# A fused attention and router kernel: the late plan one tick earlier, one GpSimd drain instead of two, later inverse norms, and one product moved to GpSimd

## The chip, the cores and the metric

The kernel runs on one core of a Trainium2 chip. The metric is device time in microseconds (us). A core has five engines with a queue each: TensorE (PE; its weight loads are shown as PEld), VectorE (DVE), ScalarE (ACT), GpSimd (POOL) and SyncE (SP, which here issues the plain DMAs). GpSimd issues the indirect DMAs, which gather or scatter rows by a list of row numbers. An engine works its queue in order; it waits on semaphores for what others make.

## The reference

Two stages. The first is a linear attention with sketched features, the second a router that sends every token to one of eight experts.

```python
# attention: q, k, v are [4, 4, 1088, 32], S1 and S2 are [8, 32]
phi(x) = outer product of (S1 x) and (S2 x), flattened to 64
kv  = einsum('bhsf,bhsd->bhfd', phi(k), v)
z   = sum over s of phi(k)
out = (phi(q) @ kv) / (phi(q) @ z + 1e-6)
# router: x = out as [4352, 128], 8 experts, hidden width 1024
xn, en  = x / (|x| + 1e-6), emb / (|emb| + 1e-6)
logits  = xn @ en.T / tau
e       = argmax(logits)
gate    = softmax(logits)[e]
out[t]  = gate[t] * (relu(x[t] @ w1[e]) @ w2[e])
```

## The kernel before

**Stages.** The four batches are worked as two halves, m = 0 and m = 1. For each half the keys of 17 groups of 128 tokens are turned, sketched and multiplied into `kp`, and summed into `kv`; then the queries are turned, sketched, multiplied into their features `qp`, and multiplied with `kv`. This gives the tokens' rows `x` and their logits, which go to a DRAM table `rows`. Each half has its queries in steps of four groups (c0 = 0, 4, 8, 12) and one of a single group (c0 = 16).

**The router in blocks.** Tokens are sorted by expert into 36 blocks of 128. Each block is gathered by an indirect DMA (`fetch`, L881), turned by TensorE (`turn`, L887, with a copy `xTb`, L889), multiplied with the expert's w1 (`up`, L935), passed through relu by ScalarE (`hT`, L943), multiplied with w2 (`down`, L971), scaled by the gate (`y`, L977) and scattered to the output by an indirect DMA (L980). In blocks 30 to 33 two experts share a block (L940, L974), with a second copy of w2 that ScalarE makes (`second_weights_b`, L922).

**The gate.** `norm` squares and sums a row on ScalarE (L948) and takes the root on GpSimd (L949, a power of 0.5). `inverse` adds a small number and takes the reciprocal on VectorE (L952, L953). `shares` is the exponential with its sum on ScalarE (L959), `share` the reciprocal of that on VectorE (L962, L963).

**Two plans.** Which token goes to which row of which block is worked out on the chip. The first plan covers m = 0 and gives blocks 0 to 9 (`EARLY` is 10), so that they can begin while m = 1's queries are still worked. The late plan covers both halves and gives blocks 10 to 35. It is made of small VectorE steps: `count` (per expert), `rest` (running sums, L814 to L823 and L700), `shared` (L829 to L844), `others` (L705 to L858), `experts` (L865 to L869), `find` (L740: compare each token's place with each row of each block), `high` and `low` (L744: two products with the digits of the token numbers). TensorE sums them (`sums`, L750, 34 small matmuls), and `tokens` (L765 to L767) makes the lists `dst_i` and `src_i` for the indirect DMAs. `first_rows` and `halves` add the blocks that two experts share. `mark` (L674) makes the table that the sums have as weights.

**Order.** It is written by hand. Every piece is put at a tick and a rank: `put_at(tick)(after, rank, f)`; the pieces are emitted by tick, then rank, and each engine gets its instructions in that order. Block i has tick 10 + i (`first` is 10), so block 10 is in tick 20 and is turned in tick 19. In tick 10 + i stand, by rank: fetch of block i + 4 (29), up (30), turn of block i + 1 (45), the inverse of some later block (46), shares (60), share (73), down of block i - 1 (74), a norm of some later block (74.6), the loads of w1 for block i + 2 (79). The late plan has ticks 13 to 18 (`table1` is 12, and it is put at `table1` + 1 to + 6). Blocks 10 to `known` + `AHEAD` are fetched right after it; those after them four ticks ahead.

**Norms.** The norm of block i stands in the tick of block i - 3, its inverse one tick later; for blocks 10 to 12 one tick ahead and in the tick of the block. The last block's norm stands at rank 29.2 of its tick, ahead of `up`.

**Drains.** In ticks 28 and 42 (blocks 18 and 32) GpSimd has a drain at rank 29.5 (L1092): it goes on only when it has nothing under way.

**Queries of m = 1.** They are placed by a table of their own: step by step `tr` (turn q), `ab` (sketch), `b` (copy of the second factor), `prod` (`features`, L385), `tr_qp` (L537), `qpT` (L542), `nd` (L550) and `x` (L560 to L567). [...] `tr_qp` and `nd` use two rotating PSUM buffers (`ps_big`), as `up` does.

Of the kernel before, what the change touches and what calls it, by code (L numbers as in the profile page):

```python
# [48 lines left out]
EARLY = (NM * NC * P // 2 - E * (P - 1) + P - 1) // P  # L49
LATE = NBLK - EARLY  # L50
SHARED = E // 2
PAIRS = FULL - EARLY
AHEAD = 4
USUAL = N // P + 2
# [9 lines left out]
def kernel(  # L64
# [13 lines left out]
    nc = tc.nc  # L78
# [8 lines left out]
    def ps_small():  # L87
        return psum.tile([P, 512], F32, tag="t", bufs=2, name="ps_t")

    def ps_big():  # L90
        return psum.tile([P, 2, 512], F32, tag="big", bufs=2, name="ps_big")
# [121 lines left out]
    ps = ps_small()  # L213
# [264 lines left out]
    def queries(m, c0, c1, put, put_nd):  # L478
        n = c1 - c0
        w = n * P  # L480
        s = {}
# [11 lines left out]
        def ab():  # L493
            s["ab"] = sketch(ab_bank(put.tick, n, 0), s["qT"], n)

        by_pool = m == 1 and c0 == 0

        def b():
            if by_pool:
# [20 lines left out]
        def seconds(j):  # L520
            if j == 0:
                s["b"] = tile_of(n, [P, 2, w], "qpT")
                s["qpT"] = held[:, c0 // 4].rearrange("p (a n) -> p a n", a=2)
            nc.scalar.copy(s["b"][:, j].rearrange("p (j n) -> p j n", j=2), s["big"][j][:, :, 2 * P:])  # L524
# [3 lines left out]
                                 s["big"][j][:, :, :2 * P].rearrange("p j (a n) -> p j a n", a=2),  # L528
                                 s["b"][:, j].rearrange("p (j a n) -> p j a n", j=2, a=2))

        def tr_qp(half=None):
            if half != 1:
                s["ps"] = ps_big() if n > 1 else ps_small().rearrange("p (b n) -> p b n", b=2)
            ps = s["ps"]
            for j in range(n) if half is None else range(2 * half, 2 * half + 2):
                for p in range(2):
                    nc.tensor.transpose(ps[:, p, j * P:(j + 1) * P],  # L537
                                        s["qp"][:, j, 2 * p:2 * p + 2].rearrange("p h f -> p (h f)"), ident)
# [31 lines left out]
        if m == 0:  # L570
            put(-1, 53, tr)
            if n == 1:
                put(0, 50, ab)
                put(0, 50.5, b)
                put(0, 54, prod)
                for f in (tr_qp, qpT):
                    put_nd(-1, 57, f)
            else:
                put(0, 50, pairs)
                for j in range(2):  # L580
                    put(0, 50.5, lambda j=j: seconds(j))
                    put(0, 54, lambda j=j: prods(j))
            put_nd(0, 70, nd)
            put_nd(0, 71.5 if n == 1 else 71, x)
        else:

            at_rank = ({tr: (7, 53), ab: (7, 70.6), b: (7, 70.7), prod: (7, 71.2), tr_qp: (8, 55.5), qpT: (8, 58),
                        nd: (8, 84), x: (8, 90)},
                       {tr: (8, 53.5), ab: (8, 55.8), b: (8, 58.7), prod: (8, 62.5), tr_qp: (9, 20), qpT: (9, 20),
                        nd: (9, 30), x: (9, 71)},  # L590
                       {tr: (8, 55.3), ab: (8, 84.6), b: (8, 84.7), prod: (9, 20.2), (lambda: tr_qp(0)): (9, 30.2),
                        (lambda: tr_qp(1)): (9, 30.22), qpT: (9, 30.6),
                        nd: (10, 70), x: (10, 71)},
                       {tr: (8, 84.5), ab: (9, 21), b: (9, 30.7), prod: (10, 33), tr_qp: (11, 20), qpT: (11, 20),
                        nd: (11, 70), x: (11, 71)})[min(step, 3)]
            for f, (t, rank) in at_rank.items():
                put_at(t)(0, rank, f)
        if c1 == s1:

            by = 1 if m == 0 else 2  # L600
            bank = (lambda: spare[m, 4 + 4 * by]) if c1 < NC else (lambda: table_bank[m][:, 0])
            best, pick, place, take, split, mark, write = router(m, s0, s1, g, bank)

            if m == 0 and c1 < NC:
                at_rank = {best: (0, 80), pick: (0, 81), place: (1, 70.5), take: (1, 71.2), split: (2, 54),
                           mark: (2, 54), write: (1, 55)}
            elif m == 0:
                at_rank = {best: (0, 80), pick: (0, 81), place: (1, 56), take: (1, 56.9), split: (1, 57),
                           write: (0, 82), mark: (1, 59)}
            elif c1 < NC:  # L610
                at_rank = {best: (1, 72), pick: (1, 72), write: (1, 90), place: (2, 70.5),
                           take: (2, 71.2), split: (4, 76.5), mark: (5, 76)}
            else:
                at_rank = {best: (1, 31), pick: (1, 31), place: (2, 31), take: (2, 32), split: (2, 32),
                           write: (1, 90), mark: (6, 32)}
            if c1 == NC:
                put_nd(at_rank[place][0], at_rank[place][1] - 0.1, lambda: table_bank.append(ps_big()))
            for f, (t, rank) in at_rank.items():
                put_nd(t, rank, f)
# [255 lines left out]
    def of(i):  # L875
        return (0, i) if i < EARLY else (1, i - EARLY)

    def fetch(i):
        t, j = of(i)
        xs[i] = work.tile([P, ROW], F32, tag="xs", bufs=AHEAD + 2, name="xs")  # L880
        nc.gpsimd.indirect_dma_start(  # L881
            out=xs[i][:], out_offset=None, in_=rows[:2 * S if t == 0 else N],
            in_offset=bass.IndirectOffsetOnAxis(ap=src_i[t][:, j:j + 1], axis=0))
# [23 lines left out]
    def two(i):  # L907
        return FULL <= i < FULL + SHARED
# [36 lines left out]
    def norm(i):  # L945
        sq = work.tile([P, DM], F32, tag="sq", bufs=1, name="sq")
        norms[i] = work.tile([P, 1], F32, tag="norm", bufs=6, name="norm")
        nc.scalar.activation(sq, xs[i][:, :DM], ACT.Square, accum_out=norms[i])  # L948
        nc.gpsimd.tensor_tensor(out=norms[i], in0=norms[i], in1=half_c, op=ALU.pow)  # L949

    def inverse(i):
        nc.vector.tensor_scalar_add(norms[i], norms[i], NORM_EPS)  # L952
        nc.vector.reciprocal(norms[i], norms[i])  # L953
# [36 lines left out]
    def put_at(tick):  # L990
        def put(after, rank, f):
            at.setdefault(tick + after, []).append((rank, len(at.get(tick + after, ())), f))
        put.tick = tick
        return put
# [15 lines left out]
    count, rest, others = plan_early()  # L1010
    find, high, low, sums, tokens, *_ = table(0, 1, lambda: early["key"])
    put = put_at(ND_AT[0][-1] + 1)
# [13 lines left out]
    first = ND_AT[0][-1] + 3  # L1026
# [3 lines left out]
    count, rest, shared, others, experts = plan_late()  # L1030
    find, high, low, sums, tokens, first_rows, halves = table(1, NM, lambda: late["key"])
    table1 = ND_AT[1][-1] + 1
    put = put_at(table1)
    put(1, 31.5, count)
    put(2, 75, rest)
    put(1, 77, shared)
    put(3, 75, others)
    put(4, 73.5, find)
    put(4, 76, high)
    put(5, 74, low)  # L1040
    put(6, 31, sums)
    put(6, 31.1, lambda: tokens(0, PAIRS))
    put(5, 78.3, experts)
    put(6, 45.1, first_rows)
    put(6, 75.1, halves)
    put(6, 75.2, lambda: tokens(PAIRS, LATE))
    known = table1 + 6 - first
    put(6, 31.2, lambda: [fetch(i) for i in range(EARLY, known + AHEAD + 1)])

    def in_ticks(b0, b1, tick):
        for i in range(b0, b1 + 1):
            put = put_at(tick + i - b0)
            if i < b1:
                put(0, 29.9, lambda i=i: second_layers(i))
                put(0, 30, lambda i=i: up(i))
            if i + 1 < b1:
                put(0, 45, lambda i=i: turn(i + 1))
            if i < b1:  # L1060
                t = max(i - (1 if EARLY <= i <= known + AHEAD else 3), b0)
                to = put_at(tick + t - b0)
                if i == 0:
                    put(-1, 30.7, lambda: norm(0))
                    put(0, 59, lambda: inverse(0))
                else:
                    to(0, 46 if i == b0 else 29.2 if i == USUAL - 1 else 74.6, lambda i=i: norm(i))
                    to(*((1, 46) if i > t else (0, 59)), lambda i=i: inverse(i))
                put(0, 60, lambda i=i: shares(i))
                put(0, 73, lambda i=i: share(i))  # L1070
            if i > b0:
                put(0, 74, lambda i=i: down(i - 1))
            if i + 2 < b1:
                put(0, 79, lambda i=i: weights(i + 2))
                if two(i + 2):
                    put(0, 79, lambda i=i: weights_b(i + 2))
                    put(1, 79, lambda i=i: second_weights_b(i + 2))
# [10 lines left out]
        if j < EARLY or j > known + AHEAD:  # L1088
            put_at(first + j - AHEAD)(0, 29, lambda j=j: fetch(j))
    in_ticks(0, USUAL, first)  # L1090
    for t in (USUAL // 2, USUAL - AHEAD):
        put_at(first + t)(0, 29.5, lambda: nc.gpsimd.drain(fusable=False))  # L1092
    emit()
    n_late = nc.values_load(late["n"][:, :], min_val=0, max_val=LATE,
                            skip_runtime_bounds_check_because="a count of blocks, of which there are no more")
    with tc.If(n_late > USUAL - EARLY):
        put = put_at(-1)
# [37 lines left out]
```

## Time and profile before

| | us |
|---|---|
| median of 3 runs (lowest to highest) | 212.54 (211.53 to 213.53) |
| the profiled execution | 211.84 |
| its span | 210.1 |
| TensorE busy | 196.7 |
| ScalarE busy | 101.8 |
| GpSimd busy | 101.3 |
| VectorE busy | 93.7 |
| 36 fetches on GpSimd, each | 1.01 |
| 36 scatters on GpSimd, each | 1.04 |
| 36 roots on GpSimd (L949), each | 0.61 |
| VectorE waiting for those roots, in all | 21.4 |
| a fetch from issue to landing, median | 4.0 |
| drains on GpSimd, as its queue shows them | 7.50 and 2.87 |

The span is the profiled stretch of the execution; about 1.8 us of the execution's time lies around it. All rows of profiles here are of that one execution. A timeline row reads: start, duration, engine, line, operation, output <- inputs, and in square brackets how long the engine stood before it and what ended this wait. A row of the table of stretches reads: the stretch, its length, then busy time (and instructions) of PE, PEld, DVE, ACT and POOL, the granted TensorE clock, the busy share of the DMA engines, and GB/s. "PEq", "POOLq" and the like are the engines' sequencers.

### The profile page before, as it was taken

The page shows a single profiled execution, that of the slowest core. Times are in us where ns is not written, and L with a number is a line of the kernel's source. Part 1 is how long each engine was busy: PE and PEld are TensorE (multiplying, and loading weights), DVE is VectorE, ACT ScalarE, POOL GpSimd, SP SyncE. Part 2 cuts the span into 40 slices and gives each one's busy share as a digit, 9 for nine tenths or more (in the row PEclk, how much of TensorE's full clock was granted, in tenths as well). Part 3 has the DMA queues.
Part 4 walks back from the last instruction along what each step waited for, and adds up shares of the span by engine and source line. Part 5 has one row for each costly group of instructions (what it writes and reads, how often), then busy time and mean ns, then how long its engine had stood idle before and what let it go on. Part 6 is the DMA issues. An engine that isn't in the chain of part 4 may idle for free.

```text
span 210.1 us, 6984 instructions
## 1 busy us (share of the span) xinstructions
PE 196.7 (94%) x2598; PEld 185.6 (88%) x2598; DVE 93.7 (45%) x403; ACT 101.8 (48%) x291; POOL 101.3 (48%) x134
## 2 busy tenths in 40 slices
PE   8999898989699999998899999997999999999991
PEld 7668797987589999997899999997999999998991
DVE  5866678989777666672014122211212222211210
ACT  2565532362283456452156465553336655674640
POOL 4101000021652667555378776715877877663323
PEclk9999999999999999999699999999999999999999
DMA  5976999992548586209546647454466787285000
GB/s 138 322 181 193 288 282 282 270 344 61 155 177 282 188 297 215 85 25 301 167 126 162 219 149 212 159 177 151 146 154 225 157 297 283 69 297 209 23 12 24
DMA packets 28160, 39.42 MB, mean 188 GB/s; under 512 B 5737, under 2 KB 21364, under 8 KB 28128
## 3 DMA queue, kind: packets, MB, share of 16 engines
q1 hardware_dynamic: 25824, 34.23, 52.5%
q0 software_dynamic: 2304, 4.74, 7.6%
q8 instruction: 22, 0.36, 0.7%
q14 instruction: 10, 0.08, 0.1%
HBM read 34.37 MB, written 4.73 MB: 186 GB/s over the span
## 4 chain that ended last, share of the span: by engine, by line
PE 68%; issue 13%; DVE 7%; DMA 4%; POOL 4%; POOLq 1%; ACT 1%; ACTq 0%
PE ps_big L935 22%; PE ps_acc L971 12%; PE ps_ab L971 10%; DMA xs<-rows,src_i 4%; PE ps_acc L432 3%; PE ps_t L352 3%; PE ps_big L550 3%; PE ps_big L515 2%; POOL out_dram L980 2%; PE ps_acc L103 2%; PE ps_ab L369 2%; PE ps_big L940 2%; PE ps_t L887 2%; POOL xs L881 1%; PE ps_acc L974 1%
## 5 line engine op out<-in xcount | busy, mean ns | idle before, releaser
L935 PE MATMUL ps_big<-xTb,wb 128*128 128x128 f32 x512 | 63.0, 276 | 1.4 <-DVE xTb L889 1.1
L935 PEld LDWEIGHTS ps_big<-xTb,wb 128*128 128x128 f32 x512 | 59.9, 192 | 2.3 <-DVE xTb L889 1.3
L980 POOL DMA_INDIRECT out_dram<-y,dst_i x36 | 37.5, 1043 | 43.8 <-ACT y L977 17.2
L943 ACT ACTIVATE hT<-ps_big 128x1024 f32<-128x1024 f32 x36 | 36.8, 1022 | 29.4 <-PE ps_big L935 28.9
L881 POOL DMA_INDIRECT xs<-rows,src_i x36 | 36.3, 1008 | 17.9 <-issue 8.4
L971 PE MATMUL ps_acc<-w_sb,hT 128*128 x256 | 32.9, 284 | 0.0
L971 PEld LDWEIGHTS ps_acc<-w_sb,hT 128*128 128x128 f32 x256 | 31.4, 200 | 0.0
L971 PE MATMUL ps_ab<-w_sb,hT 128*128 x256 | 31.2, 275 | 0.0
L971 PEld LDWEIGHTS ps_ab<-w_sb,hT 128*128 128x128 f32 x256 | 29.9, 192 | 0.0
L889 DVE COPY xTb<-ps_t 128x128 f32<-128x128 f32 x30 | 8.7, 289 | 46.3 <-PE ps_t L887 46.1
L949 POOL TENSOR_TENSOR norm<-norm,half_c 128x1 f32<-128x1 f32 x36 | 21.6, 606 | 6.8 <-ACT sq L948 6.5
L948 ACT ACTIVATE sq<-xs 128x128 f32<-128x128 f32 x36 | 10.9, 304 | 12.8 <-DMA xs<-rows,src_i 12.7
L952 DVE TENSOR_SCALAR norm<-norm 128x1 f32<-128x1 f32 x36 | 5.4, 151 | 22.5 <-POOL norm L949 21.4
L977 ACT ACTIVATE y<-ps_acc,gate 128x128 f32<-128x128 f32 x18 | 6.6, 366 | 15.0 <-PE ps_acc L971 14.0
L887 PE MATMUL ps_t<-ident,xs 128*128 128x128 f32 x36 | 10.2, 284 | 3.1 <-DMA xs<-rows,src_i 3.1
L977 ACT ACTIVATE y<-ps_ab,gate 128x128 f32<-128x128 f32 x18 | 6.6, 367 | 12.9 <-PE ps_ab L971 12.2
L962 DVE TENSOR_SCALAR gate<-gate 128x1 f32<-128x1 f32 x36 | 5.3, 148 | 16.5 <-ACT probs L959 16.4
L385 POOL TENSOR_TENSOR qp<-both 128x1024 f32<-128x1024 f32 x1 | 2.0, 1956 | 21.8 <-ACT both L380 21.8
L385 DVE TENSOR_TENSOR kp<-ps_ab,kb 128x1024 f32<-128x1024 f32 x8 | 9.7, 1215 | 3.9 <-ACT qpT L524 2.4
L959 ACT ACTIVATE probs<-xs,norm 128x8 f32<-128x8 f32 x36 | 10.6, 295 | 0.4 <-DVE norm L953 0.4
L432 PEld LDWEIGHTS ps_acc<-v,kp 128*64 128x64 f32 x256 | 8.1, 138 | 2.1 <-issue 2.0
L432 PE MATMUL ps_acc<-v,kp 128*64 128x64 f32 x256 | 9.2, 225 | 0.7 <-issue 0.7
(236 smaller groups left out, 294.0 us busy)
## 6 DMA issues: line engine op xcount, KB each, us to landing
wb<-in_moe_w_dram SPq DMA_DIRECT2D x36, 512.0 KB, 4.1
w_sb<-in_moe_w_dram SPq DMA_DIRECT2D x16, 256.0 KB, 4.9
rows<-xg SPq DMA_DIRECT2D x4, 544.0 KB, 4.6
v<-in_v_dram SPq DMA_DIRECT2D x4, 512.0 KB, 7.8
v<-in_moe_w_dram SPq DMA_DIRECT2D x4, 512.0 KB, 5.5
k<-in_k_dram SPq DMA_DIRECT2D x3, 512.0 KB, 7.3
q<-in_q_dram SPq DMA_DIRECT2D x3, 512.0 KB, 6.4
xs<-rows,src_i POOLq DMA_INDIRECT x36, 4.0
```

The lines of the kernel that those rows point to most:

```text
L385: engine.tensor_mul(t.rearrange("p j h (i k) -> p (j h) i k", i=R), ab[:, :, 0].unsqueeze(3).broadcast_to([P, n * H, R, R]), b.unsqueeze(2 ...
L432: nc.tensor.matmul(acc[m][u * HALF:(u + 1) * HALF, i, p], s["kp"][:, c - c0, h], bass.AP(tensor=vo.tensor, offset=vo.offset, ap=[list(vo.a ...
L881: nc.gpsimd.indirect_dma_start(out=xs[i][:], out_offset=None, in_=rows[:2 * S if t == 0 else N], in_offset=bass.IndirectOffsetOnAxis(ap=sr ...
L887: nc.tensor.transpose(ps[:, :P], xs[i][:, :DM], ident)
L935: nc.tensor.matmul(ps[:, u, j * P:(j + 1) * P], w[:, f * P:(f + 1) * P], x, start=True, stop=True)
L943: nc.scalar.activation(hT[i], ps, ACT.Relu)
L948: nc.scalar.activation(sq, xs[i][:, :DM], ACT.Square, accum_out=norms[i])
L949: nc.gpsimd.tensor_tensor(out=norms[i], in0=norms[i], in1=half_c, op=ALU.pow)
L959: nc.scalar.activation(p, xs[i][:, DM:], ACT.Exp, scale=norms.pop(i)[:, 0:1], accum_out=gate[i])
L971: nc.tensor.matmul(ps, h[:, f * P:(f + 1) * P], ws[0][:, f], start=f == 0, stop=f == NF - 1)
L977: nc.scalar.activation(y, ps, ACT.Copy, scale=gate.pop(i)[:, 0:1])
L980: d = nc.gpsimd.indirect_dma_start(out=out[:, :], out_offset=bass.IndirectOffsetOnAxis(ap=dst_i[t][:, j:j + 1], axis=0), in_=y[:], in_offs ...
```

## The change

Five edits of placement and engine; what is computed stays.

1. The late plan from `rest` on moves one tick earlier; `experts` moves ahead of `find`; block 10 and 11 are fetched right after the plan (`known` falls by one), block 12 in the usual place.
2. The drain in tick 28 goes; the one in tick 42 stays.
3. The inverse of a norm moves one tick later for most blocks, so that it stands two ticks after the norm. For blocks 10 and 11 norm and inverse move one tick ahead. The last block's norm moves to rank 74.6 of the tick before.
4. The queries of m = 1, c0 = 8 get their product on GpSimd, ahead of the first fetches, and their `tr_qp`, `qpT` and `nd` move to tick 9, one tick ahead, around the first block's turn. `tr_qp` is no longer cut into halves.
5. For c0 = 12 and 16 `b` and `prod` move from the end of tick 9 and from tick 10 to earlier places in tick 9.

```diff
-        by_pool = m == 1 and c0 == 0
+        by_pool = m == 1 and c0 in (0, 8)
...
-        def tr_qp(half=None):
-            if half != 1:
-                s["ps"] = ps_big() if n > 1 else ps_small().rearrange("p (b n) -> p b n", b=2)
-            ps = s["ps"]
-            for j in range(n) if half is None else range(2 * half, 2 * half + 2):
+        def tr_qp():
+            ps = s["ps"] = ps_big() if n > 1 else ps_small().rearrange("p (b n) -> p b n", b=2)
+            for j in range(n):
...
-                       {tr: (8, 55.3), ab: (8, 84.6), b: (8, 84.7), prod: (9, 20.2), (lambda: tr_qp(0)): (9, 30.2),
-                        (lambda: tr_qp(1)): (9, 30.22), qpT: (9, 30.6),
-                        nd: (10, 70), x: (10, 71)},
-                       {tr: (8, 84.5), ab: (9, 21), b: (9, 30.7), prod: (10, 33), tr_qp: (11, 20), qpT: (11, 20),
+                       {tr: (8, 55.3), ab: (8, 84.6), b: (8, 84.7), prod: (8, 84.8), tr_qp: (9, 21.5), qpT: (9, 21.6),
+                        nd: (9, 30.3), x: (9, 71.5)},
+                       {tr: (8, 84.5), ab: (9, 21), b: (9, 21.2), prod: (9, 30.8), tr_qp: (11, 20), qpT: (11, 20),
...
-                           write: (1, 90), mark: (6, 32)}
+                           write: (1, 90), mark: (5, 32)}
...
     put(1, 31.5, count)
-    put(2, 75, rest)
     put(1, 77, shared)
-    put(3, 75, others)
-    put(4, 73.5, find)
-    put(4, 76, high)
-    put(5, 74, low)
-    put(6, 31, sums)
-    put(6, 31.1, lambda: tokens(0, PAIRS))
-    put(5, 78.3, experts)
-    put(6, 45.1, first_rows)
-    put(6, 75.1, halves)
-    put(6, 75.2, lambda: tokens(PAIRS, LATE))
-    known = table1 + 6 - first
-    put(6, 31.2, lambda: [fetch(i) for i in range(EARLY, known + AHEAD + 1)])
+    put(1, 78, rest)
+    put(2, 75, others)
+    put(2, 75.5, experts)
+    put(3, 73.5, find)
+    put(3, 76, high)
+    put(4, 74, low)
+    put(5, 31, sums)
+    put(5, 31.1, lambda: tokens(0, PAIRS))
+    put(5, 45.1, first_rows)
+    put(5, 75.1, halves)
+    put(5, 75.2, lambda: tokens(PAIRS, LATE))
+    known = table1 + 5 - first
+    put(5, 31.2, lambda: [fetch(i) for i in range(EARLY, known + AHEAD + 1)])
...
-                t = max(i - (1 if EARLY <= i <= known + AHEAD else 3), b0)
+                t = max(i - (2 if EARLY <= i <= known + AHEAD else 4 if i == USUAL - 1 else 3), b0)
...
-                    to(0, 46 if i == b0 else 29.2 if i == USUAL - 1 else 74.6, lambda i=i: norm(i))
-                    to(*((1, 46) if i > t else (0, 59)), lambda i=i: inverse(i))
+                    to(0, 46 if i == b0 else 74.6, lambda i=i: norm(i))
+                    to(*((2, 46) if i > t + 2 else (1, 46) if i > t else (0, 59)), lambda i=i: inverse(i))
...
-    for t in (USUAL // 2, USUAL - AHEAD):
-        put_at(first + t)(0, 29.5, lambda: nc.gpsimd.drain(fusable=False))
+    put_at(first + USUAL - AHEAD)(0, 29.5, lambda: nc.gpsimd.drain(fusable=False))
```

## The prediction

> **What bounds the kernel now.** I read the page's busy shares and 40 slices first, then the chain that ended last in order of time, then each engine's timeline around the places where that chain leaves TensorE, and at last tables of busy time and clock over short stretches there.
>
> ```profile
> PE 196.7 (94%) x2598; PEld 185.6 (88%) x2598; DVE 93.7 (45%) x403; ACT 101.8 (48%) x291; POOL 101.3 (48%) x134
> ...
> PEclk9999999999999999999699999999999999999999
> ```
>
> TensorE is busy 94% of the span, and its clock is full in all slices but one. From 66 us on a block costs 3.68 us of TensorE (up 1.79, down 1.79, transpose 0.11: up begins at 79.87, 83.56, 87.24). So only TensorE's gaps, and that one slow slice, can be won. The chain in order of time names them:
>
> ```profile
> 51.80 4.75 DMA xs<-rows,src_i
> ...
> 93.49 2.62 issue
> 96.12 0.19 issue
> 96.31 4.43 DMA xs<-rows,src_i
> 100.78 0.33 PE ps_t L887
> 101.11 3.40 PE ps_acc L971 x16
> 104.52 1.83 PE ps_big L935 x16
> ...
> 135.25 1.07 POOLq L1092
> ```
>
> Three places: the first fetch of rows, the fetch of block 10 (the first that needs the late plan), and the drain before block 18. At the second, TensorE ends up(9) at 98.7 and stands until 100.78, 2.1 us; then one down takes 3.40 us in place of 1.79. The table of stretches says why, and shows that the gap before the first block did not do this:
>
> ```profile
> 55.00:56.00 1.00, 0.33 (x4) 0.09 (x1) 0.96 (x3) 0.00 (x0) 0.70 (x2) 1.00 0.23 57
> ```
> ```profile
> 103.00:104.00 1.00, 1.00 (x7) 1.00 (x6) 0.00 (x0) 0.00 (x0) 0.00 (x0) 0.50 0.29 70
> ```
>
> The third column from the right is the granted clock: 0.50 after 2.1 us of idling, 1.00 through the 1.27 us before 56.6. The late gap costs 2.1 + 1.6 = 3.7 us in all. What fed it is on VectorE and TensorE:
>
> ```profile
> 87.34 1.36 DVE L740 TENSOR_TENSOR hit<-at,place_k 128x1152 bf16<-128x1152 f32 x1
> 88.74 1.36 DVE L744 TENSOR_TENSOR col<-hit,digits 128x1152 bf16<-128x1152 bf16 x1
> ...
> 91.26 1.34 DVE L744 TENSOR_TENSOR col<-hit,digits 128x1152 bf16<-128x1152 bf16 x1
> ```
> ```profile
> 92.71 2.18 PE L750 MATMUL ps_t<-col,row 128*128 128x64 bf16 x34
> ...
> 146.15 2.05 PE L935 MATMUL ps_big<-xTb,wb 128*128 128x128 f32 x16 [1.09 <-DVE xTb L889]
> ```
>
> The second column table ends at 92.6, just as TensorE is free for the sums (92.71). The drain's cost is the wait in the last row: 1.2 us between the end of down(16) and up(18).
>
> **The change part by part.**
>
> *Late plan one block sooner.* The sums go from tick 18 to tick 17, the fetches of blocks 10 and 11 with them; block 10's transpose stays in tick 19. Take before's clock. In tick 17 TensorE is free for the sums at 89.03. Is VectorE? Its work from 76.60 (shared) to the end of the second col at 92.60 is 16.0 us, of which 3.45 us are waits (0.44, 0.65, 0.44, 0.39, 0.88 and 0.65, on L949's and L959's results). One tick's inverse and gate rows (0.65) drop out, experts (0.7) comes in ahead. The gates' probs are ready at 79.6, 83.3 and 87.0, before I reach them, and norm results no longer hold it (below). So VectorE runs through: 76.6 + 16.0 - 3.45 - 0.65 + 0.7 = 89.2, with collisions 89.6. The sums begin there: a new wait of 0.6 us, in which turn(8), down(6) and everything of TensorE's queue behind the sums stands. Sums end at 91.6, src_i at 92.2; fetch 10 follows by the 0.8 us seen before (95.53 to 96.31), so 93.0, and lands 4.43 us later, at 97.4. TensorE reaches turn(10) after turn(8), down(6), up(8), turn(9), down(7), up(9), four times 1.8 us and the transposes, at 99.1. That is 1.7 us of slack: both the wait and the half clock go. Gain 3.7 - 0.6 = 3.1 us; bounds of the new wait 0.2 and 2.0. On GpSimd's queue fetches 10 and 11 now stand ahead of out(6), which needs y only at 93.9; fetch 12 moves to the head of tick 18 behind out(6), lands near 101 and is wanted by a transpose at 106. On SP nothing moves; the expert numbers of late blocks come 10 us earlier.
>
> *One drain.* The first drain kept GpSimd from 137.50 to 142.78, out(16), norm and fetch 23 behind it; VectorE stood 5.38 us at `norm` with the transpose's copy behind it.
>
> ```profile
> 136.49 1.01 POOL L881 DMA_INDIRECT xs<-rows,src_i  x1 [0.17 <-issue]
> 143.65 1.02 POOL L980 DMA_INDIRECT out_dram<-y,dst_i  x1 [6.15 <-issue]
> ```
>
> Without it these follow at their usual 3.68 us: gain 1.2 us. Lower bound 0, if GpSimd must do the same waiting unasked. The kept drain held GpSimd 2.29 us (193.15 to 195.44); I keep that value.
>
> *Inverse norms.* L952 and L953 of block i move from tick i-2 to i-1, still ahead of its exp in tick i. Nothing is added. The 21.4 us that VectorE waits for L949 mostly vanish; they hid under TensorE except behind the drain. Worth 0 alone.
>
> *Norm of the last block.* ACT's sq(35) moves from ahead of relu(32) to ahead of the copy of w2 for block 32.
>
> ```profile
> 188.40 1.03 ACT L922 COPY v<-w_sb 128x1024 f32 x1
> 192.12 0.31 ACT L948 ACTIVATE sq<-xs 128x128 f32<-128x128 f32 x1 [2.69 <-DMA xs<-rows,src_i]
> 192.43 1.00 ACT L943 ACTIVATE hT<-ps_big 128x1024 f32<-128x1024 f32 x1
> ```
>
> It waits for fetch 35 until 192.1. Now the copy (1.03) stands behind that wait and relu(32) behind the copy, so hT(32) is ready at 194.6 in place of 193.4; down(32) began at 194.17. Loss 0.5 us; 0 if the fetch lands 0.5 us earlier, 1.0 if as much later.
>
> *Third queries' product on GpSimd.* VectorE loses 1.21 us (L385), ACT's copy grows from 0.27 to 0.37, GpSimd gains the 1.96 us of the row at 41.51 for the same shape. ACT can copy at 49.47, so GpSimd works 49.9 to 51.9; fetch 0, issued at 51.80, now queues behind it: 52.2, 0.4 us late. Then TensorE: tr_qp of step 2 at 53.2 (it waits for its bank, which x of step 0 reads until 53.07), nd of step 1 to 55.5, idle until the rows land at 57.0, transpose, nd of step 2 (1.29) beside ACT's copy, up(0) at 58.5. Before, up(0) began at 57.34 but nd (1.29) followed it, and 0.29 us of waiting. The next up begins at 61.9 in place of 62.29: gain 0.4 us. Bounds -0.8 and +0.9.
>
> [...] In this trace VectorE's rows beside GpSimd's product (41.5 to 43.5) keep their usual durations, L562 0.69 us as elsewhere; but place_k (L666), from SBUF to SBUF beside an indirect DMA at 75.05, took 0.39 in place of 0.17, and out_dram beside hit and col 1.5 to 1.7 us in place of 1.0. [...] The chain's first row is the nearest, I take 0.4.
>
> [...]
>
> **Sum**: 3.1 + 1.2 - 0.5 + 0.4 = 4.2 us. The profiled execution took 211.84 us (span 210.1 and 1.8 around it), so 207.6; the median of the runs is 0.7 above it: 208.3 us.
>
> **Rivals.**
>
> *The plan is not ready (0.13).* VectorE's col ends 2 us late: collisions with GpSimd (hit and col take two SBUF inputs) and the gates' waits return. For it: the 0.2 us of place_k, and that I left no waits in 13 us of VectorE. Against: hit and col kept 1.36 beside GpSimd before. TensorE then idles 2 us at the sums and the half clock may follow: 3.1 becomes 1.7 or 0.1, time 209.7 to 211.3.
>
> *The start slips (0.10).* The idle time before the first transpose grows from 1.27 to near 2 us, and the clock falls there: 0.6 more delay and 1.6 of half clock: 210.5.
>
> *The kept drain pays for both (0.09), slower.* The first drain came after 40 GpSimd DMAs (23 fetches, 17 outs) and held 5.28 us, the second after 27 more and held 2.29. That is 0.0033 and 0.0031 us per DMA squared; with 67 behind one drain it would hold 14.4 us. From out(31) at 196.34 to out(35) at 206.48 five outs of 1.3 us leave 5.0 us of room, so 7.3 us of hold are free and each us beyond lengthens the end; the time of before is passed from 11.5 us on (7.3 and the 4.2 gained). At 14.4: 207.6 + 7.1 + 0.7 = 215.4. Against: rows fetched at 136.49 landed near 140.5, and both holds may be a wait for landings, which does not grow.
>
> **How the numbers follow.** The forecast has 0.62, with 207.4 to 209.4 as its own range; 0.06 is left for what I don't see, half of it near 212.5. One per cent, what a measurement here can tell from no change, is 2.1 us: 210.4 and 214.7. Faster: 0.62, half of the second rival, most of the first's lower half, and a little: 0.77. Slower: 0.09. The range 206.8 to 210.9 holds the forecast with its bounds, and most of the two middle rivals.
>
> **What would show it.** Right: PEclk full in every slice; no wait of L887 for xs at block 10 and fetch 10 issued some 6 us before block 10's transpose is due; a wait below 1 us at L750 on col; no up behind an xTb held by a norm; the one DRAIN near 3 us. Wrong: a slice of PEclk below 9, a DRAIN above 7 us, a GpSimd gap over 5 us elsewhere, or L935 of block 1 starting later than 62.3 us.

## The result, and the profile after

| | before | after |
|---|---|---|
| median of the runs, us | 212.03 (211.44 to 213.53, 4 runs) | 205.26 (204.68 to 205.70, 4 runs) |
| profiled execution, us | 211.84 (span 210.1) | 205.20 (span 203.4) |
| mean granted clock there | 0.992 | 0.997 |

The ratio is 0.9669, 95% interval 0.9609 to 0.9729: faster, by more than forecast, and the time lies below the forecast range. A later comparison (its experiment is below) gave 210.79 and 205.79 us, ratio 0.9731, 0.9629 to 0.9833. The ratios here and below are those on record for the fast runs, so they are not the quotients of the medians beside them.

The page of the profile after, busy shares (part 1) and granted clock (part 2):

```profile
PE 194.1 (95%) x2598; PEld 183.3 (90%) x2598; DVE 91.8 (45%) x402; ACT 101.9 (50%) x291; POOL 103.5 (51%) x135
...
PEclk9999999999999999999999999999999999999998
```

The one slow slice is gone; the 8 is the last slice, in which TensorE has finished. TensorE is busy 2.6 us less, although it computes the same: in the profile before, it ran at half clock for 3.4 us, which accounts for 1.7 of the 2.6.

The front, on the timelines of TensorE, VectorE and GpSimd (start, duration, engine, line; in brackets the idle time before and its releaser). Behind the edit in `tr_qp`, lines stand two lower in number than before, and from the edit of the table of m = 1's queries on three lower: L932 is the up matmul, L884 the transpose of a block, L548 nd, L535 tr_qp.

```profile
52.33 1.06 PE L535 MATMUL ps_big<-ident,qp 128*128 128x128 f32 x8 [0.46 <-ACT qpT L540]
53.32 1.36 PE L548 MATMUL ps_big<-kz,qpT 128*64 128x82 f32 x32
54.61 0.33 PE L884 MATMUL ps_t<-ident,xs 128*128 128x128 f32 x1
54.87 1.36 PE L548 MATMUL ps_big<-kz,qpT 128*64 128x82 f32 x32
56.22 2.02 PE L932 MATMUL ps_big<-xTb,wb 128*128 128x128 f32 x16
```

```profile
50.29 0.62 DVE L764 TENSOR_SCALAR src_i<-dst_i 128x10 int32<-128x10 int32 x1
```

```profile
48.94 1.95 POOL L385 TENSOR_TENSOR qp<-both 128x1024 f32<-128x1024 f32 x1 [6.34 <-ACT both L380]
51.22 1.21 POOL L878 DMA_INDIRECT xs<-rows,src_i  x1 [0.33 <-DVE c_early L791]
```

The transpose of block 0 has no bracket: fetch 0, issued at 51.22, had landed by 54.61, 3.4 us later, where it took 4.8 before. The second nd now stands ahead of up(0). On VectorE src_i takes 0.62 us in place of 0.17, and ends (50.91) as GpSimd's product ends (50.89).

The late plan, TensorE and GpSimd:

```profile
86.93 2.17 PE L747 MATMUL ps_t<-col,row 128*128 128x64 bf16 x34
```

```profile
90.55 1.01 POOL L878 DMA_INDIRECT xs<-rows,src_i  x1 [2.14 <-issue]
```

The sums start 0.3 us after up(7) has ended, so they hardly wait for VectorE's col; fetch 10 goes out 5.8 us earlier than before (96.31), and no transpose waits for its rows any more.

The end, on ScalarE and GpSimd:

```profile
183.71 0.31 ACT L945 ACTIVATE sq<-xs 128x128 f32<-128x128 f32 x1 [2.41 <-DMA xs<-rows,src_i]
...
184.19 1.05 ACT L919 COPY v<-w_sb 128x1024 f32 x1
185.14 1.02 ACT L940 ACTIVATE hT<-ps_big 128x1024 f32<-128x1024 f32 x1
```

```profile
191.25 1.05 POOL L977 DMA_INDIRECT out_dram<-y,dst_i  x1 [6.52 <-issue]
```

The copy of w2 stands between the wait for fetch 35 and hT(32), as the diff says. GpSimd idles 6.5 us around the one drain, 3.2 us around the second drain before (the DRAIN instruction itself takes 6.20 us in place of 2.87).

Where the 6.65 us of span came from (210.06 less 203.41), by the start of up(i), the first matmul of block i with w1, in both profiles (before minus after, and what each stretch added):

| stretch | us before minus after at its end | added |
|---|---|---|
| start, to fetch 0 without its slip by the product | 1.03 | 1.03 |
| front, to up(2) | 2.67 | 1.64 |
| plan, to up(20) | 5.85 | 3.18 |
| first drain, to up(22) | 7.21 | 1.36 |
| end, to up(34) and the last out | 6.65 | -0.56 |

The first row is code that the change does not touch.

### The profile page after: what moved, and what is told of

Same layout as the page of the kernel before. It is cut to its first block, busy times and chain, and to the rows that moved or that the text cites. A ratio compares the mean times of both kernels' runs of the same rounds, so it can differ in the third digit from the quotient of the medians.

```text
span 203.4 us, 6991 instructions
## 1 busy us (share of the span) xinstructions
PE 194.1 (95%) x2598; PEld 183.3 (90%) x2598; DVE 91.8 (45%) x402; ACT 101.9 (50%) x291; POOL 103.5 (51%) x135
## 4 chain that ended last, share of the span: by engine, by line
PE 67%; DVE 10%; issue 9%; DMA 4%; ACT 4%; POOL 3%; POOLq 1%; SPq 0%; ACTq 0%; DVEq 0%
PE ps_big L932 22%; PE ps_acc L968 11%; PE ps_ab L968 11%; PE ps_acc L432 4%; DMA xs<-rows,src_i 4%; PE ps_big L548 4%; PE ps_t L352 3%; PE ps_ab L369 2%; POOL out_dram L977 2%; PE ps_big L515 2%; PE ps_t L884 2%; PE ps_big L535 2%; DVE col L741 1%; DVE kp L385 1%; PE ps_t L747 1%
## 5 line engine op out<-in xcount | busy, mean ns | idle before, releaser
L932 PE MATMUL ps_big<-xTb,wb 128*128 128x128 f32 x512 | 63.0, 276 | 0.0
L932 PEld LDWEIGHTS ps_big<-xTb,wb 128*128 128x128 f32 x512 | 59.7, 192 | 0.8 <-ACT xTb L886 0.2
L968 PE MATMUL ps_acc<-w_sb,hT 128*128 x256 | 31.3, 275 | 0.0
L968 PEld LDWEIGHTS ps_acc<-w_sb,hT 128*128 128x128 f32 x256 | 29.9, 192 | 0.0
L385 POOL TENSOR_TENSOR qp<-both 128x1024 f32<-128x1024 f32 x2 | 3.9, 1955 | 27.7 <-ACT both L380 27.7
L884 PE MATMUL ps_t<-ident,xs 128*128 128x128 f32 x36 | 10.2, 282 | 0.0
L354 ACT COPY kT<-ps_t 128x512 f32<-128x512 f32 (+1 forms) x10 | 5.2, 526 | 6.3 <-PE ps_t L352 5.9
```

Source lines behind the costliest of these rows:

```text
L385: engine.tensor_mul(t.rearrange("p j h (i k) -> p (j h) i k", i=R), ab[:, :, 0].unsqueeze(3).broadcast_to([P, n * H, R, R]), b.unsqueeze(2 ...
L884: nc.tensor.transpose(ps[:, :P], xs[i][:, :DM], ident)
L932: nc.tensor.matmul(ps[:, u, j * P:(j + 1) * P], w[:, f * P:(f + 1) * P], x, start=True, stop=True)
L968: nc.tensor.matmul(ps, h[:, f * P:(f + 1) * P], ws[0][:, f], start=f == 0, stop=f == NF - 1)
```

## The experiments

Eight kernels ran: four put one part each into the kernel before, and four took one part out of the changed kernel, or nothing. Each was timed beside the kernel before; a comparison's interval reaches 0.5 to 1.9% to each side, so the places in the traces say more than the medians. The starts of up(i), in us, from the timeline of each profile ("tr" is the first transpose of the second queries' product, tr_qp; the start before it is the same code in all but for the product on GpSimd):

```
            tr     fetch0  up(0)  up(1)  up(2)  up(7)  up(10)  up(20)  up(21)  up(32)  up(34)
before     51.07   51.80   57.34  62.29  68.14  87.24  104.31  141.22  146.15  187.63  196.18
after      50.04   51.22   56.22  59.35  65.47  84.84   98.54  135.37  139.05  180.42  189.54
plan       50.26   50.98   58.27  63.22  69.07  88.17  101.57  138.40  143.52  185.75  194.41
drain      52.22   52.95   60.25  66.80  72.64  92.24  108.27  145.09  148.78  190.94  199.21
product    50.90   52.07   59.38  62.51  68.63  87.73  104.73  142.17  147.24  189.51  198.49
norms      50.68   51.40   58.74  65.29  71.14  90.24  105.38  142.20  145.89  187.99  196.46
same       50.52   51.69   56.69  59.83  65.95  85.05   98.44  135.27  138.95  180.33  189.60
no product 50.95   51.68   56.04  60.99  66.84  85.94   99.34  136.16  139.84  181.21  189.54
2 drains   52.55   53.73   58.73  61.86  67.98  87.08  100.49  137.31  140.99  182.36  191.06
last norm  53.19   54.37   59.37  62.51  68.66  87.77  101.17  138.00  141.68  183.05  191.67
```

**One part each, in the kernel before.** The kernel before beside these four: 216.16 us (212.94 to 221.62, 19 runs). That is 5.4 us more than beside the last four, which ran later and on another chip of the machine, so times of the two groups are not compared with each other.

The plan alone:

```diff
-    put(6, 31, sums)
+    put(5, 31, sums)
...
-    known = table1 + 6 - first
+    known = table1 + 5 - first
```

> The kernel of before with the late plan one tick earlier and nothing else. Additive theory (each part is worth what its place in the profile of after shows): 3.2 us faster than before, up(10) begins 3.2 us earlier counted from up(2), no slice of the clock below 9, the wait at the sums (L750) near 0.3 us. Rival (the plan needs the later inverses, because VectorE still stands at norms of GpSimd in ticks 13 to 16): the sums wait over 1 us and the gain is 2.5 us or less.

212.60 us (210.08 to 215.59), ratio 0.9775, 0.9654 to 0.9895. From up(7) to up(10) it takes 13.40 us where the kernel before takes 17.07: 3.67 us, the 2 us of idling and the 1.7 us of half clock behind it. The sums do not wait: up(8) follows up(7) by 5.93 us, as in all other kernels with the early plan but the first profile after (6.24). The theory holds.

The first drain alone removed:

```diff
-    for t in (USUAL // 2, USUAL - AHEAD):
-        put_at(first + t)(0, 29.5, lambda: nc.gpsimd.drain(fusable=False))
+    put_at(first + USUAL - AHEAD)(0, 29.5, lambda: nc.gpsimd.drain(fusable=False))
```

> The kernel of before without its first drain and nothing else. Additive theory: 1.3 us faster, all of it at up(21), and the kept drain's hold of GpSimd grows from 2.3 us after its last instruction to about 5.7 as in the profile of after, without moving the end. Rival (the drain's waiting comes back unasked): a GpSimd gap of 3 us or more elsewhere before block 32, gain under 0.5 us. Its code up to block 17 is that of before, so its first fetch shows whether 4.8 us from issue to the first transpose is usual: if the late packet of one DMA engine is chance, it lands in 3.5 to 4.2 us here and up(0) begins about 1 us earlier than in the profile of before.

214.17 us (212.99 to 215.65), ratio 0.9840, 0.9728 to 0.9952. up(21) follows up(20) by 3.69 us in place of 4.93: 1.24 us, as expected, and GpSimd's idle time at the kept drain grows from 3.19 to 6.47 us without moving the end (the last out starts 10.3 us after up(34) there, as before). Its first transpose is on record 3.4 us after fetch 0 was issued, with no wait for it, though up(0) is late for another reason (see the next run).

The third queries' product and stage alone, with edit 5 of the change, which goes with it:

```diff
-        by_pool = m == 1 and c0 == 0
+        by_pool = m == 1 and c0 in (0, 8)
...
-                       {tr: (8, 55.3), ab: (8, 84.6), b: (8, 84.7), prod: (9, 20.2), (lambda: tr_qp(0)): (9, 30.2),
+                       {tr: (8, 55.3), ab: (8, 84.6), b: (8, 84.7), prod: (8, 84.8), tr_qp: (9, 21.5), qpT: (9, 21.6),
...
```

> The kernel of before with the product of c0 = 8 on GpSimd and its stage ahead of the first block, and nothing else. Theory A (the early gain of the profile of after is mostly the luck of the first fetch and of the input loads): 0.2 to 0.6 us faster, first up(2) at a fixed distance of 27 to 28 us from the first nd of m = 1, and a start (first TensorE work on queries of m = 1) anywhere within 1 us. Theory B (the early gain of 2.7 us is caused by the moved product): about 2.5 us faster.

215.39 us (213.86 to 219.31), ratio 0.9990, 0.9935 to 1.0044: no difference that can be told. In the profile neither expectation could be read, because something else came in. In all four profiles of this comparison up(0) starts 7.3 us after fetch 0 is issued, whatever the order of the stage, where the two first profiles have 5.54 and 5.00. The profile with the later norms shows it on TensorE and ScalarE:

```profile
54.77 0.27 PE L887 MATMUL ps_t<-ident,xs 128*128 128x128 f32 x1
54.88 0.60 PE L537 MATMUL ps_big<-ident,qp 128*128 128x128 f32 x4
58.74 2.42 PE L935 MATMUL ps_big<-xTb,wb 128*128 128x128 f32 x16 [3.26 <-ACT qpT L542]
```

```profile
57.34 0.27 ACT L889 COPY xTb<-ps_t 128x128 f32<-128x128 f32 x1 [4.52 <-remote]
```

The transpose is on record at 54.77, but ScalarE, which copies its result, starts 2.6 us later, released by an event that the profile can only call remote; VectorE is released with it. The pages of these four profiles give no landing time for any DMA, those of the other six do, so the word may only mean that the profile lacks the record. What the stall is stays open: it came in four of four profiles there and in none of the six others, whatever part was in. The kernel before, without any part, was 5.4 us slower in that comparison too, so the stall most likely belongs to that chip or that hour; no profile of the kernel before was taken there, which would have shown it.

The later inverses and the move of the last block's norm alone:

```diff
-                t = max(i - (1 if EARLY <= i <= known + AHEAD else 3), b0)
+                t = max(i - (2 if EARLY <= i <= known + AHEAD else 4 if i == USUAL - 1 else 3), b0)
...
-                    to(*((1, 46) if i > t else (0, 59)), lambda i=i: inverse(i))
+                    to(*((2, 46) if i > t + 2 else (1, 46) if i > t else (0, 59)), lambda i=i: inverse(i))
```

> The kernel of before with the later inverses and the last block's norm ahead of the copy of w2, and nothing else. Additive theory: 0.5 us slower at up(34) from the last block's norm; at the first drain it gains, since the transpose's copy no longer stands behind a held norm: up(21) is late by 0 to 0.5 us in place of 1.2, so in sum 0 to 0.7 us faster. Rival (the order of norms changes nothing at the drain): 0.5 us slower than before.

216.88 us (212.13 to 219.91), ratio 0.9956, 0.9766 to 1.0147. The median says nothing, the trace does: up(21) follows up(20) by 3.69 us although both drains stand. The later inverses alone take the first drain's loss away. The same profile shows what the stall at the front does to the clock. Busy time by stretch, the granted clock third from the right:

```profile
60.00:61.00 1.00, 1.00 (x8) 0.97 (x7) 0.51 (x2) 0.00 (x0) 0.90 (x1) 0.60 0.01 4
61.00:62.00 1.00, 1.00 (x12) 0.70 (x12) 0.52 (x3) 0.80 (x1) 0.00 (x0) 0.50 0.29 70
62.00:63.00 1.00, 1.00 (x19) 1.00 (x18) 0.00 (x0) 0.97 (x6) 0.12 (x1) 0.50 0.00 0
63.00:64.00 1.00, 1.00 (x15) 0.83 (x12) 0.17 (x1) 0.62 (x4) 1.00 (x3) 0.69 0.00 0
```

After 3.26 us of idling the clock is halved for 3.4 us, and up(1) comes 6.55 us after up(0) in place of 4.95. The profile with the plan alone has the same stall (3.2 us) and a full clock. So a gap of this length had the half clock behind it in one execution and not in another; what decides was not shown.

**One part out of the changed kernel.** The kernel before beside these four: 210.79 us (209.55 to 213.42, 7 runs).

The changed kernel itself:

> The changed kernel as it is, so that the kernels with one part taken back are read against it on one chip. If the start before 45 us and the landing of fetch 0 are chance, fetch 0 is issued anywhere from 51.2 to 53.4 us, and up(0) begins either 5.0 us after it (as in the changed kernel's first profile) or 7.3 us after it (as in the four profiles with one part each); if the change made the first profile's quick front, it is 5.0 again. In both cases: no half clock before the end except, perhaps, at the front; sums wait near 0.3 us; no loss at up(21).

205.79 us (205.07 to 206.86), ratio 0.9731, 0.9629 to 0.9833. Fetch 0 to up(0) is 5.00 us again, and 5.00 in the two kernels below that share its front, so the stall of the one-part comparison is not the change's. The sums do not wait (5.93), and up(6) and up(7), which the first profile after had 0.27 us late, are on time. From tr to up(2) it takes 15.43 us, to the hundredth as in the first profile after.

Without the product part (VectorE multiplies the third queries, and their stage stands behind up(0), by the diff of the product reversed):

> The change without its third part (third queries' product back on VectorE, their stage back behind up(0)). Theory: nd and transposes that stood between up(0) and up(1) fill the wait for fetch 0, whatever its length: without it, issue of fetch 0 to up(2) is 1.5 us longer than in a_same at equal length of the wait, fetch 0 is issued 0.4 us earlier, and as the plan no longer waits, the whole 1.1 us stays to the end (and 1.7 us more in executions in which the longer idling halves the clock). Rival: the 1.6 us of the first pair of profiles was the luck of one late packet, and the part is worth the 0.4 us forecast or less: the kernels lie within 0.5 us.

205.93 us (205.02 to 207.07), ratio 0.9739, 0.9634 to 0.9844: level with the changed kernel. On TensorE:

```profile
54.54 0.66 PE L537 MATMUL ps_big<-ident,qp 128*128 128x128 f32 x4
55.04 0.27 PE L887 MATMUL ps_t<-ident,xs 128*128 128x128 f32 x1
55.15 0.60 PE L537 MATMUL ps_big<-ident,qp 128*128 128x128 f32 x4
56.04 2.02 PE L935 MATMUL ps_big<-xTb,wb 128*128 128x128 f32 x16 [0.29 <-issue]
```

This is the front of the kernel before, and here its transpose does not wait: fetch 0, issued at 51.68, has landed by 55.04, 3.4 us later. From tr to up(2) it takes 15.89 us. The part is worth 15.89 - 15.43 = 0.46 us, and the theory (1.1 us) is wrong: it took the stage's shift (issue of fetch 0 to up(2) is 15.16 us here against 14.26, 0.90 us and not 1.5) from profiles with longer waits. The kernel before took 17.07 us over the same stretch with the same order; 1.18 us of that was one late packet. The rival is right.

With the drain of block 18 kept:

```diff
-    put_at(first + USUAL - AHEAD)(0, 29.5, lambda: nc.gpsimd.drain(fusable=False))
+    for t in (USUAL // 2, USUAL - AHEAD):
+        put_at(first + t)(0, 29.5, lambda: nc.gpsimd.drain(fusable=False))
```

> The change with the drain of block 18 kept. Theory of the sum (the parts add up): the drain again costs 1.2 to 1.4 us at up(21), and the hold of the second drain falls from 5.6 us to some 2.3. Rival, from the kernel with the later inverses alone, in which both drains stood and up(21) followed up(20) by 3.69 us: the drain delayed TensorE only through VectorE's inverses, which now come a tick later, so up(21) is less than 0.3 us late and the time is that of the changed kernel.

205.25 us (204.27 to 206.72), ratio 0.9676, 0.9576 to 0.9776, nothing lost. GpSimd, VectorE and TensorE around the drain:

```profile
139.83 1.01 POOL L977 DMA_INDIRECT out_dram<-y,dst_i  x1 [6.23 <-DVE xTb L886]
140.85 0.58 POOL L946 TENSOR_TENSOR norm<-norm,half_c 128x1 f32<-128x1 f32 x1
```

```profile
139.41 0.29 DVE L886 COPY xTb<-ps_t 128x128 f32<-128x128 f32 x1 [2.11 <-PE ps_t L884]
141.47 0.15 DVE L949 TENSOR_SCALAR norm<-norm 128x1 f32<-128x1 f32 x1 [1.77 <-POOL norm L946]
```

```profile
140.99 1.95 PE L932 MATMUL ps_big<-xTb,wb 128*128 128x128 f32 x16
```

In the kernel before, VectorE had at this place:

```profile
145.31 0.15 DVE L952 TENSOR_SCALAR norm<-norm 128x1 f32<-128x1 f32 x1 [5.38 <-POOL norm L949]
...
145.83 0.27 DVE L889 COPY xTb<-ps_t 128x128 f32<-128x128 f32 x1
```

GpSimd is held 6.2 us, as in the kernel before (6.15), and VectorE still waits for a norm of GpSimd. But xTb, which TensorE needs for up(21), now stands ahead of that waiting instruction and is copied at 139.41, 1.6 us before up(21); before, it stood behind it and was copied at 145.83, 0.3 us before up(21). The rival is right: the removal and the later inverses cure the same loss, and either is enough.

With the last block's norm back at its old place:

```diff
-                t = max(i - (2 if EARLY <= i <= known + AHEAD else 4 if i == USUAL - 1 else 3), b0)
+                t = max(i - (2 if EARLY <= i <= known + AHEAD else 3), b0)
...
-                    to(0, 46 if i == b0 else 74.6, lambda i=i: norm(i))
+                    to(0, 46 if i == b0 else 29.2 if i == USUAL - 1 else 74.6, lambda i=i: norm(i))
...
```

(The line at the last dots keeps this block's inverse one tick behind its norm, as before.)

> The change with the last block's norm back at its old place, ahead of the copy of w2. Forecast's term: 0.5 us faster than a_same, seen between up(30) and up(34). Rival: GpSimd's hold by the drain or the copy on ScalarE sets the end anyway, and the two agree within 0.2 us at up(34).

206.44 us (204.83 to 207.34), ratio 0.9722, 0.9618 to 0.9826: no gain. On ScalarE, first in the changed kernel's second profile, then here:

```profile
184.61 0.31 ACT L945 ACTIVATE sq<-xs 128x128 f32<-128x128 f32 x1 [3.41 <-DMA xs<-rows,src_i]
...
185.08 1.05 ACT L919 COPY v<-w_sb 128x1024 f32 x1
186.03 1.02 ACT L940 ACTIVATE hT<-ps_big 128x1024 f32<-128x1024 f32 x1
```

```profile
187.48 0.31 ACT L945 ACTIVATE sq<-xs 128x128 f32<-128x128 f32 x1 [2.62 <-DMA xs<-rows,src_i]
...
187.79 1.00 ACT L940 ACTIVATE hT<-ps_big 128x1024 f32<-128x1024 f32 x1
```

The mechanism is there: hT(32) starts 1.42 us after the waiting sq with the copy between them, 0.31 without. From up(32) to up(34) the five profiles with the old order take 8.27 to 8.98 us (mean 8.62), the five with the new order 8.33 to 9.27 (mean 8.78). The 0.16 us between the means lie well inside either spread, to which the landing of fetch 35 adds (the square of its rows starts 4.1 to 6.0 us after its issue). Whether the move costs anything is not settled.

Not tried: the changed kernel without any drain, the third product on VectorE with its stage still ahead of the first block, the removed drain without the later inverses in the changed kernel, and a second profile of the kernel before.

## Why the prediction missed

The direction and most of the mechanisms were right, the time was 3.0 us too long. The step that failed is the term of the front, and what stood under it: "idle until the rows land at 57.0", with fetch 0 landing 4.8 us after its issue because it did so in the profile before. In the profile after, TensorE took up its rows 3.4 us after the issue, at 54.61, and did not idle. The late landing was an accident of one execution. By the sum's own terms, against the profiled executions (207.6 forecast, 205.2 measured):

- **Start, forecast at 0: 1.03 us.** The sum took the time of fetch 0 in the profile before as fixed. Less the 0.45 us that the product adds where it runs on GpSimd, fetch 0 went out between 50.8 and 53.9 us in the ten profiles, with no relation to the change. 51.80 was neither early nor late, and the profile after was the earliest: luck.
- **Product, forecast +0.4: 1.64 between the two profiles.** The part itself is 0.46, as said, by the steps given (the stage moved ahead of up(0), less the slip of the fetch). The other 1.18 is the late packet in the profile before. The sum carried it over into the changed kernel.
- **Plan, forecast +3.1: 3.18.** In the first profile after, the sums waited 0.3 us where 0.6 was forecast, and up(6) and up(7) came 0.27 us late, for which the sum had no term; in the later profiles of the changed kernel neither happened, and then it is 3.7. So the closeness of 3.18 is in part luck. And 1.7 of it is the half clock, which the gap does not always bring: of the seven runs of the kernel before in the later comparison, three at a mean clock of 0.999 or more took 209.55 to 210.42 us, four at 0.987 to 0.992 took 210.79 to 213.42.
- **Drain, forecast +1.2: 1.36.** Right in size, wrong in its owner. "Worth 0 alone" for the inverses did not see that they bring xTb out from behind the waiting norm. They are worth the same 1.24 us at up(21) alone, and the two together no more (1.36 is counted to up(22)). The sum came out right only since one was set to 0.
- **Last block's norm, forecast -0.5: -0.56 over the end in the first pair,** but as much chance as the start: over five profiles each, -0.16, well inside the scatter.

These differ from the forecast by 1.03, 1.24, 0.08, 0.16 and -0.06, 2.45 in all, which is the 2.4 between 207.6 and 205.2. The remaining 0.6 is the step from the profile to the median: 0.7 was added since the median before stood that far above its profile, and after it stood 0.06 above.

The range failed for the same reason. Its bounds held the costs of the change, but nothing for the profile before being itself one draw: 1.03 and 1.18 us of the gain were that.

Added up without the accidents, the runs give plan 3.7 (or 2.0 in an execution without the half clock), drain or inverses 1.24, product 0.46, last norm about 0: 5.4 or 3.7 us. The later comparison, with both kinds of executions in it, shows 5.0.

The rivals: the plan was ready, so the first is out. Of the second, the slip of the fetch came (0.45 us: fetch 0 goes out 1.18 us after tr with the product on GpSimd and 0.73 without; src_i took 0.62 us beside the product and, in the profile after, ended with it, at 50.91 and 50.89; it took 0.17 in the kernels without it), but TensorE did not idle, having the second nd to do. For the third, the hold did grow, from 3.2 to 6.5 us of idle time, but not with the square of the DMAs: it was 3.2 to 6.0 after 27 of them, 5.9 to 6.3 after 40 and 6.5 after 67, and the end did not move (up(34) to the last out is 10.3 us with one drain or two). The forecast had kept 2.29 us for this hold, by the second drain before: too small by more than half, and harmless.

## What to carry to other kernels

Before a stall in a profile is put into a sum, ask whether the change's own instructions make it, or a transfer that landed late once; a second profile of the same kernel tells. When two edits remove the same wait (here the drain that held GpSimd, and the instruction that waited for GpSimd ahead of a needed copy), count it once, and look first at the order on the engine that waits: moving one instruction there cost nothing and was enough. A part that moves work into a wait is worth what is left of the wait on an ordinary run.

## What the runs showed of the hardware

- **The half clock followed some of the gaps.** Four profiles have it before the end. In three of them tables of stretches show its edges: it lasted 3.4 us at 0.50 (norms: from 60.2 to 63.6, by the rows further up; drain: from 61.0 to 64.4; before: from 101.1 to 104.5), and so cost 1.7 us of full-speed matmuls. It followed gaps of 1.9 to 3.3 us, but not each of them: the stall of 3.2 to 3.3 us at the front had it in two profiles (norms, drain) and not in a third (plan), the gap of 1.9 to 2.0 us at block 10 in two (before, product) and not in a third (drain). Here are the gap at the front of the plan kernel, which kept its full clock, and then those at block 10 of the product kernel and of the drain kernel, each with the down behind it:

```profile
54.45 0.60 PE L537 MATMUL ps_big<-ident,qp 128*128 128x128 f32 x4
58.27 2.02 PE L935 MATMUL ps_big<-xTb,wb 128*128 128x128 f32 x16 [3.21 <-DVE parts L566]
```

```profile
101.73 0.33 PE L884 MATMUL ps_t<-ident,xs 128*128 128x128 f32 x1 [2.01 <-DMA xs<-rows,src_i]
101.90 3.04 PE L968 MATMUL ps_acc<-w_sb,hT 128*128 x16
```

```profile
106.28 0.33 PE L887 MATMUL ps_t<-ident,xs 128*128 128x128 f32 x1 [1.98 <-DMA xs<-rows,src_i]
106.45 1.98 PE L971 MATMUL ps_acc<-w_sb,hT 128*128 x16
```

  A gap of 2 us thus cost 2 us in the drain kernel, and 3.7 us, the 1.7 of the half clock with it, in the kernel before. What decides which was not shown.
- **Fetch 0 was as late as its last packet.** The transpose of its rows is on record 3.4 us after its issue in the nine other profiles, and 4.8 us after it in the profile before, where fifteen of its sixteen landings are on record from 54.36 to 54.89 us, the last at 56.56, and the transpose starts at 56.60. Why that one was late is not known.
- **The stall of the one-part comparison.** TensorE before up(0), ScalarE and VectorE were held until 5.8 to 5.9 us after fetch 0 was issued, in four different kernels, and in none of the six other profiles. It is the largest difference between two executions that these runs have: 2.3 to 3.0 us at up(0) between kernels with the same front, and 1.6 more with the half clock. Its cause is open; that the kernel before was 5.4 us slower there as well speaks for the chip or the hour, and against any part of the change.
